# Linear attention into an MLP on one core: a rebuilt front, and every attention step placed by itself

## The chip, the cores and the metric

The kernel runs on one core of a Trainium2 chip. The metric is device time in microseconds, as the median of several runs. The profile shows one execution. Its engines are TensorE (PE for matmuls, PEld for loading weights), VectorE (DVE), ScalarE (ACT), GpSimd (POOL) and SyncE (SP), which here only issues transfers. Each engine takes its instructions in the order in which the program lists them.

## What is computed

There are two parts, and the second takes the output of the first.

```python
def phi(x):                                        # S1, S2: 8 x 32
    a = np.einsum('rd,bhsd->bhsr', S1, x)
    b = np.einsum('rd,bhsd->bhsr', S2, x)
    return np.einsum('bhsi,bhsj->bhsij', a, b).reshape(*x.shape[:-1], 64)
q_p, k_p = phi(q), phi(k)                          # q, k, v: 4 x 4 x 1088 x 32
kv = np.einsum('bhsf,bhsd->bhfd', k_p, v)
z = np.sum(k_p, axis=2)
x = (q_p @ kv) / (q_p @ z + 1e-06)                 # then 4352 tokens x 128
h = x @ w_in                                       # 128 x 2048
out = (h * sigmoid(beta * h)) @ w_out              # 2048 x 128
```

## The kernel before

Attention is done batch by batch. For each of the four batches the steps are these, with the lines of the kernel before:

- `load_k`, `load_q`, `load_v`: transfers from DRAM. `hold` (L115) first writes one column of the target on an engine, which makes the transfer wait for that place in the program. All but the first k and beta are issued on SP.
- `k_turn` (L287) and `q_turn` (L293): VectorE transposes blocks of 32x32, so that the head dimension lies along partitions.
- `project` (L314 on TensorE, L323 on VectorE): the product with S1 and S2, then a transpose back into a tile `ab`.
- `k_product` (L343): the 64 features of k, shared between VectorE and GpSimd.
- `v_copy` (L304): v with a column of ones, for kv and z at once.
- `kv` (L362), `kv_spread` (L372, L376), `weights` (L386, L394), `kv_repeat` (L403 on TensorE, L411 on ScalarE): the sums over all tokens, brought into the shapes that the later products need.
- `den_product`, `den_invert`, `weigh` (L418 on TensorE, L428 to L462 on VectorE): the denominators, and a tile `an` of q's first factor divided by them.
- `q_multiply` (L479) and `q_back` (L487), for three thirds (`ch` 0, 1, 2): the 64 features of q, then a transpose.
- `num_part` (L498), and the copies of its result into `x_all` (L556), two on VectorE and two on ScalarE.

The sequence is divided into 34 units of 32 tokens in each batch. The MLP (`moe`) takes ten chunks of 12, 11, 11, six times 16, and 6 units. A chunk runs as a series of waves: two matmuls with `winp` (L605) fill a pair of PSUM banks, ScalarE applies Silu to both (L612) into `gT`, and two waves later two matmuls with `woutp` (L581) add to the output (four and four for the last chunk). There are two pairs of banks, so wave n+2 needs the pair that ScalarE has read for wave n. There are 76 waves; here they are counted from 0. Chunks 0 to 2 (waves 0 to 23) belong to batch 0, and batch 1 must be ready for wave 24, batch 2 for wave 40, batch 3 for wave 56. `winp` is w_in times beta and `woutp` is w_out over beta; GpSimd makes them in steps of two blocks (L255, L264).

Batch 0 is written out ahead of the waves, with its own form of the first third: its numerator is formed undivided (`num_first`) and multiplied by the reciprocals later (`quotient`, L530, L539), so that wave 0 needs one third of the batch alone. Between the steps stand idle matmuls on a zero tile (`warm`, L210). The later batches' steps are attached to waves by number: `at_wave(n, f)` puts f behind wave n in the program. Most steps come in groups, for example

```python
at_wave(w0 + proj_k, *((a.v_copy,) if b > 1 else ()), a.k_project, a.k_product)
at_wave(w0 + wt, a.weights, a.kv_repeat)
at_wave(w0 + den, a.weigh)
at_wave(w0 + n0, lambda a=a: a.num_part(0, NCH, EV))
```

No scheduler moves anything: this order is what each engine runs.

Of the kernel before, what the change touches and what calls it, by code (L numbers as in the profile page):

```python
# [7 lines left out]
F32 = mybir.dt.float32  # L8
F16 = mybir.dt.float16
ALU = mybir.AluOpType  # L10
# [8 lines left out]
def kernel(  # L19
# [32 lines left out]
    assert U == 34  # L52
# [45 lines left out]
    s16 = const.tile([2 * R, D], F32, tag="s16")  # L98
# [8 lines left out]
    nc.scalar.dma_start(out=k_in[0], in_=k_rows[0])  # L107
    nc.sync.dma_start(out=s16[0:R, :], in_=S1)
    nc.sync.dma_start(out=s16[R : 2 * R, :], in_=S2)
    nc.scalar.dma_start(out=beta4[0:P:T, :], in_=moe_beta.rearrange("(i n) -> i n", n=512))  # L110
    nc.sync.dma_start(out=q_in[0], in_=q_rows[0])
# [5 lines left out]
    def load_w_in(eng):  # L117
        hold(eng, w_in_sb)
        nc.sync.dma_start(out=w_in_sb, in_=moe_w_in)
        nc.sync.dma_start(out=betat, in_=moe_beta.rearrange("(p j) -> p j", j=NJ))  # L120
# [5 lines left out]
    def load_k(b, eng):  # L126
        hold(eng, k_in[b])
        nc.sync.dma_start(out=k_in[b], in_=k_rows[b])
# [29 lines left out]
    for h in range(H):  # L158
        nc.gpsimd.memset(hmask[T * h : T * h + T, h % 2, :], 1.0)

    j8 = const.tile([2 * R, P // R, R], F32, tag="j8")
    nc.gpsimd.memset(j8, 1.0)
    nc.gpsimd.affine_select(
        out=j8, in_=j8, pattern=[[0, P // R], [-1, R]], base=-R, channel_multiplier=1,
        compare_op=ALU.is_equal, fill=0.0,
    )
# [6 lines left out]
    load_v_late(0, nc.gpsimd)  # L173
# [32 lines left out]
    idle_out = bank("acc")  # L206

    def warm(n):
        for _ in range(n):
            nc.tensor.matmul(out=idle_out, lhsT=idle[:, 0:P], rhs=idle, start=True, stop=True)  # L210
# [7 lines left out]
    def sketches():  # L218

        w = bank("att")  # L220
        for h in range(H):
            nc.tensor.matmul(
                out=w[T * h : T * h + T, 0 : 2 * R], lhsT=s16, rhs=idf[0 : 2 * R, 0 : 2 * R], start=True, stop=True
            )
        nc.vector.tensor_tensor(
            out=apx(wab, 0, [[2 * R, 2], [1, 2 * R]]),
            in0=apx(w, 0, [[0, 2], [1, 2 * R]]),
            in1=hmask,
            op=ALU.mult,
        )  # L230
        w = bank("att")
        nc.tensor.matmul(out=w[:, 0:D], lhsT=j8.rearrange("k x r -> k (x r)"), rhs=s16, start=True, stop=True)
        nc.scalar.copy(out=s2rep, in_=apx(w, 0, [[0, H], [1, D]]))
# [6 lines left out]
    def beta_rows():  # L240

        for i in range(2):
            w = pair()
            for k_ in range(2):
                p0 = T * (2 * i + k_)
                nc.tensor.matmul(
                    out=w[:, k_, :], lhsT=ones[p0 : p0 + 1, :], rhs=beta4[p0 : p0 + 1, :], start=True, stop=True
                )
            nc.scalar.copy(
                out=beta_bc[:, 1024 * i : 1024 * i + 1024].rearrange("q (k n) -> q k n", k=2), in_=w  # L250
            )

    def scale_w_in(j0, j1):
        for j in range(j0, j1, 2):
# [3 lines left out]
                in1=apx(beta_bc, j, [[1, 2], [NJ, P]]),  # L258
                op=ALU.mult,
            )  # L260

# [15 lines left out]
    class Attention:  # L277
# [5 lines left out]
        def k_turn(self, halves=(0, 1)):  # L283
            half = U // 2 + 1
            for i in halves:
                u0, u1 = ((0, half), (half, U))[i]
# [10 lines left out]
        def v_copy(self):  # L297
            if self.first:
                parts = ((nc.scalar.copy, 0, 2), (nc.scalar.copy, 2, H))
            else:  # L300
                parts = ((nc.gpsimd.tensor_copy, 0, H),)
            for f, h0, h1 in parts:
                for p1, c0, c1 in ((P, 0, NL), (T * (NS - 1), NL, C)):
                    f(  # L304
                        out=self.vc[0:p1, c0:c1, h0:h1, 0:D].rearrange("p c h d -> p h c d"),
                        in_=v_in[self.b][0:p1, h0:h1, c0:c1, :],
                    )
# [438 lines left out]
```

## Time and profile before

| What | Value |
|---|---|
| Median of 3 runs | 112.78 us (112.75 to 115.35) |
| Profiled execution: its own time | 112.65 us |
| its span (first to last instruction) | 110.8 us |
| TensorE matmul busy | 101.1 us, 91% |
| VectorE busy | 69.5 us, 63% |
| ScalarE busy | 75.7 us, 68% |
| GpSimd busy | 30.7 us, 28% |
| Mean granted clock of TensorE | 0.985 |

The time of the profiled execution is 1.85 us more than its span, which begins with the first instruction and ends with the last. TensorE's busy time is large in part because matmuls overlap and idle matmuls count as well. Stages are therefore read from tables by stretch and from the chain of work that ended last, which goes back from the last instruction, each time to what released it.

Some durations that are needed below, as means of one instruction: L612 at 1024 columns 1059 ns, 704 columns 756 ns, and in sequence about 0.1 us less each, since they overlap; L343 on GpSimd 1067 ns for 512 elements and 3061 ns for 768; L479 about 930 ns; L487 974 ns; L255 1070 ns; L264 622 ns; L293 1305 ns.

### The profile page before, as it was taken

What the parts mean: (1) busy time and instruction counts of PE and PEld (TensorE: products, weight loads), DVE (VectorE), ACT (ScalarE), POOL (GpSimd) and SP (SyncE); (2) the same over time, 40 slices, a digit from 0 to 9 for tenths busy, and PEclk for the clock granted to TensorE, in tenths of its full rate; (3) what the DMA queues carried; (4) which work ended last, traced back from release to release, by engine and by line L of the source; (5) the groups of instructions that cost most, each with busy time, mean ns of one, the idle gap of its engine ahead of it and who ended that gap; (6) DMA issues with size and microseconds to landing.
All of it is one profiled execution on the core that took longest, in us unless ns stands there. A gap on an engine that the chain in (4) does not pass through costs nothing.

```text
span 110.8 us, 3276 instructions
## 1 busy us (share of the span) xinstructions
PE 101.1 (91%) x1385; PEld 49.5 (45%) x1385; DVE 69.5 (63%) x137; ACT 75.7 (68%) x105; POOL 30.7 (28%) x54
## 2 busy tenths in 40 slices
PE   5999796987988999899999999999999999999950
PEld 2332763334456555444734443365444444444640
DVE  5269775899998799579769965933998220020110
ACT  1608411292753799479569976856999799999940
POOL 6503197899580003228000040920000000000000
PEclk9999999599999999999999999999999999999999
DMA  3899139997001342249401506060000056004153
GB/s 91 261 264 313 65 62 400 387 268 272 11 0 24 53 131 70 37 64 356 90 6 35 167 3 101 0 92 9 0 0 0 16 85 96 1 12 65 24 74 56
DMA packets 22119, 11.25 MB, mean 101 GB/s; under 512 B 18772, under 2 KB 20820, under 8 KB 21848
## 3 DMA queue, kind: packets, MB, share of 16 engines
q1 hardware_dynamic: 21536, 10.42, 37.3%
q10 hardware_dynamic: 568, 0.61, 1.8%
q8 instruction: 11, 0.18, 0.7%
q14 instruction: 4, 0.03, 0.1%
HBM read 8.80 MB, written 2.23 MB: 99 GB/s over the span
## 4 chain that ended last, share of the span: by engine, by line
PE 39%; DVE 28%; ACT 18%; DMA 5%; issue 2%; POOL 2%; SPq 1%; ACTq 0%; POOLq 0%; DVEq 0%
ACT gT L612 17%; PE wave L605 10%; PE acc L581 9%; DVE qpt L487 8%; DVE qp L479 6%; DMA v_in<-in_v_dram 5%; PE wave L498 4%; PE att L418 3%; PE att L314 2%; PE att L362 2%; PE att L403 2%; PE wave L362 2%; DVE kp L343 2%; DVE den L444 2%; PE att L498 1%
## 5 line engine op out<-in xcount | busy, mean ns | idle before, releaser
L612 ACT ACTIVATE gT<-wave 128x1024 f16<-128x1024 f32 (+2 forms) x76 | 65.1, 958 | 11.7 <-PE wave L605 11.6
L605 PE MATMUL wave<-x_all,winp 128*128 128x512 f16 (+3 forms) x160 | 42.5, 353 | 0.3 <-ACT gT L612 0.3
L581 PE MATMUL acc<-gT,woutp 128*128 128x512 f16 (+3 forms) x160 | 41.7, 347 | 0.2 <-ACT gT L612 0.2
L605 PEld LDWEIGHTS <-winp 128*128 128x128 f16 x160 | 14.2, 99 | 21.6 <-issue 13.0
L581 PEld LDWEIGHTS <-woutp 128*128 128x128 f16 x160 | 15.3, 97 | 14.4 <-issue 0.4
L586 DVE STREAM_TRANSPOSE osb<-acc 128x512 f32<-128x512 f32 (+3 forms) x10 | 6.2, 618 | 16.8 <-PE acc L581 16.8
L343 POOL TENSOR_TENSOR kp<-ab 128x768 f32<-128x768 f32 (+1 forms) x4 | 10.3, 2563 | 13.1 <-DVE ab L323 13.1
L487 DVE STREAM_TRANSPOSE qpt<-qp 128x768 f32<-128x768 f32 x12 | 11.7, 974 | 0.4
L304 POOL COPY vc<-v_in 128x896 f32<-128x896 f32 (+1 forms) x6 | 4.2, 740 | 22.3 <-DMA v_in<-in_v_dram 22.3
L210 PE MATMUL acc<-idle 128*128 128x512 f16 x23 | 8.3, 500 | 1.3 <-DVE idle L145 1.3
L498 PE MATMUL wave<-qpt,kvw 32*32 32x288 f32 (+2 forms) x192 | 6.9, 344 | 1.9 <-DVE qpt L487 1.9
L479 DVE TENSOR_TENSOR qp<-an,ab 128x768 f32<-128x768 f32 x9 | 8.4, 930 | 0.1
L255 POOL TENSOR_TENSOR winp<-w_in_sb,beta_bc 128x256 f16<-128x256 f32 x8 | 8.4, 1070 | 0.0
L323 DVE STREAM_TRANSPOSE ab<-att 128x288 f32<-128x288 f32 x16 | 6.6, 453 | 2.3 <-PE att L314 2.3
L343 DVE TENSOR_TENSOR kp<-ab 128x1536 f32<-128x1536 f32 (+2 forms) x5 | 7.3, 1481 | 0.2
L287 DVE STREAM_TRANSPOSE kT<-k_in 128x576 f32<-128x576 f32 (+1 forms) x8 | 5.5, 717 | 1.9 <-DMA k_in<-in_k_dram 1.8
L411 ACT COPY kvw<-att 128x128 f32<-128x128 f32 x8 | 2.1, 267 | 6.3 <-PE att L403 5.9
L556 ACT CAST x_all<-att 128x288 f16<-128x288 f32 (+1 forms) x8 | 2.6, 382 | 5.4 <-PE att L498 5.4
L556 DVE CAST x_all<-wave 128x288 f16<-128x288 f32 (+1 forms) x8 | 3.1, 428 | 4.6 <-PE att L498 4.6
L498 PE MATMUL att<-qpt,kvw 32*32 32x288 f32 (+1 forms) x128 | 6.0, 392 | 0.0
L498 PEld LDWEIGHTS wave<-qpt,kvw 32*32 32x32 f32 x192 | 3.8, 103 | 4.6 <-ACT gT L612 3.3
L293 DVE STREAM_TRANSPOSE qT<-q_in 128x1088 f32<-128x1088 f32 x4 | 5.2, 1305 | 0.1
(85 smaller groups left out, 76.1 us busy)
## 6 DMA issues: line engine op xcount, KB each, us to landing
q_in<-in_q_dram SPq DMA_DIRECT2D x4, 544.0 KB, 6.6
v_in<-in_v_dram SPq DMA_DIRECT2D x12, 144.0 KB, 5.7
k_in<-in_k_dram SPq DMA_DIRECT2D x3, 544.0 KB, 4.1
w_in_sb<-in_moe_w_in_dram SPq DMA_DIRECT2D x1, 1024.0 KB
w_out_sb<-in_moe_w_out_dram SPq DMA_DIRECT2D x1, 1024.0 KB, 4.8
out_dram<-osb SPq DMA_DIRECT2D x16, 64.0 KB, 2.0
k_in<-in_k_dram ACTq DMA_DIRECT2D x1, 544.0 KB, 3.6
v_in<-in_v_dram SPq DMA_DIRECT2D x4, 112.0 KB, 4.3
```

Of the source, the lines that this page charges most:

```text
L210: nc.tensor.matmul(out=idle_out, lhsT=idle[:, 0:P], rhs=idle, start=True, stop=True)
L255: nc.gpsimd.tensor_tensor(out=winp[:, j : j + 2, :], in0=apx(w_in_sb, j, [[1, 2], [NJ, P]]), in1=apx(beta_bc, j, [[1, 2], [NJ, P]]), op=AL ...
L323: nc.vector.transpose(out=apx(ab, T * p, [[2 * T, C], [1, T]]), in_=banks[p][:, 0 : C * T])
L343: eng.tensor_tensor(out=apx(self.kp, c0 * H * F, [[F, n], [R, R], [1, R]]), in0=apx(t, c0 * H * 2 * R, [[2 * R, n], [1, R], [0, R]]), in1= ...
L479: nc.vector.tensor_tensor(out=apx(self.qp, 0, [[F, n], [R, R], [1, R]]), in0=a, in1=apx(self.ab, c0 * H * 2 * R + R, [[2 * R, n], [0, R], ...
L487: nc.vector.transpose(out=apx(self.qpt, ch * CW * T, [[T, CW], [C * T, 2 * H], [1, T]]), in_=self.qp.rearrange("p n f -> p (n f)"),)
L498: nc.tensor.matmul(out=dst[T * h : T * h + T, 0:n], lhsT=self.kvw[T * s : T * s + T, h % 2, fb, h // 2, :], rhs=self.qpt[T * s : T * s + T ...
L556: copies[e](out=x[:, :, s * CT : (s + 1) * CT], in_=src.rearrange("p (c n) -> p c n", n=CT))
L581: nc.tensor.matmul(out=acc[:, :n], lhsT=woutp[:, j, :], rhs=gT[:, j, :n], start=(j == 0), stop=(j == NJ - 1))
L586: nc.vector.transpose(out=osb[:, :un, :].rearrange("p u m -> p (u m)"), in_=acc[:, :n])
L605: nc.tensor.matmul(out=wave[:, jj // (nj // 2), jj % (nj // 2) * n : (jj % (nj // 2) + 1) * n], lhsT=winp[:, j0 + jj, :], rhs=x, start=Tru ...
L612: nc.scalar.activation(out=gT[:, j0 : j0 + nj, :n].rearrange("p (i k) n -> p i k n", i=2), in_=wave[:, :, : nj // 2 * n].rearrange("p i (k ...
```

## The change

The front:

- S1 and S2 are brought in by two transfers that repeat the 8 rows over all 128 partitions. A transpose on VectorE and a product with the mask then give `wab`. The matmuls that did this (L222, L232) and the tile `j8` are gone.
- The first k is loaded in halves on SP, followed by q and v on the same queue; v no longer waits for a mark on GpSimd. ScalarE's queue issues S and beta. The first half of batch 1's k is also loaded early, ahead of w_in; the other half later.
- Idle matmuls have 320 columns in place of 512, and their numbers change. The 192 columns left free in that PSUM bank take the rows of batch 0's second denominator.
- `project` runs in two parts for batch 0's k. `k_product` is called for each engine by itself; batch 0's q transpose stands between the two VectorE parts.
- Batch 0's v is copied on ScalarE (units 0 to 3) and GpSimd (4 to 8), all heads at once.
- The copies of beta are laid out so that GpSimd reads them contiguously; ScalarE reads PSUM with a stride for that.
- `q_back(0)` is done before `kv_spread`. `kv_repeat` is split around the new `den_rows`, which is the matmul part of `den_product`. `num_first` and `quotient` go by pairs of banks. Half of batch 1's k transpose stands in the front.
- Eight of the sixteen `woutp` blocks are made on ScalarE, two each after waves 1 to 4.

The later steps: a table `plan` gives every step of every batch a place of its own, and a step with value p stands behind wave floor(p), in the order of the values. `num_part` is divided into the matmuls and `evacuate`. Batch 1's second `q_multiply` runs on GpSimd. Batch 0's last copies go three to ScalarE and one to VectorE (`AVAA`).

```diff
+    UH = U // 2 + 1
+    nc.sync.dma_start(out=k_in[0][:, 0 : UH * D], in_=k_rows[0][:, 0 : UH * D])
+    for i, s_ in enumerate((S1, S2)):
+        nc.scalar.dma_start(
+            out=s12[:, i, :], in_=bass.AP(tensor=s_.tensor, offset=s_.offset, ap=[[0, P // R], [D, R], [1, D]])
+        )
+    nc.sync.dma_start(out=k_in[0][:, UH * D : U * D], in_=k_rows[0][:, UH * D : U * D])
+    nc.sync.dma_start(out=q_in[0], in_=q_rows[0])
     nc.scalar.dma_start(out=beta4[0:P:T, :], in_=moe_beta.rearrange("(i n) -> i n", n=512))
-    nc.sync.dma_start(out=q_in[0], in_=q_rows[0])
+    load_v(0)
...
+    NI = 512 - 2 * CT
     def warm(n):
         for _ in range(n):
-            nc.tensor.matmul(out=idle_out, lhsT=idle[:, 0:P], rhs=idle, start=True, stop=True)
+            nc.tensor.matmul(
+                out=idle_out[:, 0:NI], lhsT=idle[:, 0:P], rhs=idle[:, 0:NI], start=True, stop=True
+            )
...
+        st = const.tile([P, 2, T], F32, tag="st")
+        nc.vector.transpose(out=st.rearrange("p i r -> p (i r)"), in_=s12.rearrange("p i d -> p (i d)"))
...
+        nc.scalar.copy(
+            out=apx(beta_bc, i * half, [[P, NJ], [1, half]]),
+            in_=apx(beta_ps[i], 0, [[1, NJ], [NJ, half]]),
+        )
...
+    def scale_w_out_act(j):
+        nc.scalar.activation(out=woutp[:, j, :], in_=w_out_sb[:, j, :], func=ACTF.Copy, scale=rbetat[:, j : j + 1])
...
-    warm(9)
+    warm(15)
     a0.k_turn((0,))
     sketches()
-    warm(2)
+    a0.k_project((0, 1))
+    load_k(1, nc.vector, 0, UH)
+    load_w_in()
+    warm(1)
     a0.k_turn((1,))
-    load_w_in(nc.vector)
-    a0.k_project()
+    a0.k_project((2, 3))
+    beta_rows(0)
+    beta_rows(1)
+    beta_copy(0)
+    warm(7)
+    a0.k_product(nc.vector, 0, 4)
+    hold(nc.vector, w_outf)
+    hold(nc.gpsimd, w_outf)
     a0.q_turn()
-    beta_rows()
-    warm(5)
-    a0.v_copy()
-    a0.k_product()
+    a0.k_product(nc.gpsimd, 7, C)
+    a0.k_product(nc.vector, 4, 7)
+    a0.v_copy(nc.scalar.copy, ((0, 4),))
+    a0.v_copy(nc.gpsimd.tensor_copy, ((4, 7), (7, 9)))
+    beta_copy(1)
     a0.q_project()
-    warm(3)
+    warm(4)
     a0.kv((0, 1))
     a0.q_multiply(0)
-    hold(nc.vector, w_outf)
-    hold(nc.gpsimd, w_outf)
+    load_w_out(nc.vector)
+    a0.q_back(0)
     scale_w_in(0, 10)
+    warm(2)
+    load_k(1, nc.vector, UH, U)
     a0.kv_spread()
-    load_w_out(nc.vector)
-    warm(2)
+    load_q(1, nc.vector)
     a0.weights()
-    a0.kv_repeat()
...
+    a0.kv_repeat((0,))
+    a0.den_rows(0, 1)
+    a0.kv_repeat((1,))
+    at[1].k_turn((0,))
     a0.den_product(0, 1)
     a0.den_invert(0, 1, rz[:, :, 0:H])
     a0.spread_rden()
+    nc.vector.reciprocal(out=rbetat, in_=betat)
+    a0.num_first()
+    warm(3)
+    a0.quotient()
     load_v_late(1, nc.vector)
-    a0.num_first()
-    a0.quotient()
+    a0.den_rows(1, NCH, idle_out[:, NI:512])
+    warm(3)
     a0.den_product(1, NCH)
     a0.weigh(1)
-    warm(2)
     for j in range(10, NJ, 2):
         scale_w_out(j - 10, j - 8)
         scale_w_in(j, j + 2)
-    scale_w_out(NJ - 10, NJ)
-    at[1].v_copy()
...
+    slots = [(1.5 + (j - NJ // 2) // 2, -1, lambda j=j: scale_w_out_act(j)) for j in range(NJ // 2, NJ)]
+    plan = [
+        {"mul1": 0.1, "back1": 0.45, "mul2": 0.15, "back2": 0.5, "num": 4.05, "ev": 4.1},
+        {"turn_k": 0.6, "proj_k": 5.1, "vcopy": 0.1, "kp_pool": 7.5, "turn_q": 1.6, "kp": 5.75, "proj_q": 7.3, "kv0": 9.1, "kv1": 9.5, "spread": 9.6, "weights": 9.65, "repeat": 10.5, "den": 10.15, "inv": 10.2, "mul0": 13.45, "back0": 16.1, "mul1": 17.2, "back1": 19.8, "mul2": 17.55, "back2": 19.85, "num": 22.9, "ev": 22.95},
+        {"load_k": 1, "load_q": 1.05, "load_v": 13.3, "turn_k": 8.1, "turn_q": 10.55, "vcopy": 23.4, "proj_k": 20.95, "kp_pool": 24.4, "kp": 21.7, "proj_q": 23.6, "kv0": 25.05, "kv1": 25.25, "spread": 25.6, "weights": 26.05, "repeat": 31.1, "den": 28.9, "inv": 29.4, "mul0": 29.85, "back0": 32.3, "mul1": 30.5, "back1": 32.35, "mul2": 32.95, "back2": 35.7, "num": 38.5, "ev": 38.85},
+        {"load_k": 16, "load_q": 21.1, "load_v": 32.2, "turn_k": 26.6, "turn_q": 24.85, "vcopy": 39.6, "proj_k": 33.75, "kp_pool": 36.6, "kp": 39, "proj_q": 39, "kv0": 41.25, "kv1": 41.9, "spread": 41.95, "weights": 43.3, "repeat": 45.5, "den": 44.05, "inv": 46.65, "mul0": 46.7, "back0": 48.75, "mul1": 47.75, "back1": 50.8, "mul2": 49.8, "back2": 51, "num": 54, "ev": 54.95},
+    ]
...
+            "ev": lambda a=a, b=b: a.evacuate("VVAA" if b else "AVAA"),
...
+            do[f"mul{ch}"] = lambda a=a, ch=ch, e=nc.gpsimd if b == 1 and ch == 1 else None: a.q_multiply(ch, e)
...
     n = 0
     for u0, un in chunks:
         for _ in moe(u0, un):
-            for f in slots.get(n, ()):
-                f()
             n += 1
+            while slots and slots[0][0] < n:
+                slots.pop(0)[2]()
     flush(0)
```

In the kernel before, the places of the later batches in the same counting were: batch 1: k turn 2, proj_k 5, proj_q 7, kv and weights with repeat 9, denominators 10, q's products 14, numerator 22. Batch 2: proj_k 23, proj_q 25, kv 27, weights with repeat 28, denominators 29, q's products 32, numerator 38. Batch 3: proj_k 39, proj_q 41, kv 43, weights with repeat and denominators 44, q's products 46 and 48, numerator 54.

## The prediction

> **What bounds the kernel now.** I read the slices of the span first, to see where the clock or the transfers are unusual; then the chain that ended last, for who sets the time; then tables of busy time by stretch, for what each stage could still give.
>
> ```profile
> PEclk9999999599999999999999999999999999999999
> DMA  3899139997001342249401506060000056004153
> ...
> 10.76 1.25 ACT vc L304 x3
> 12.01 0.04 issue
> 12.05 2.17 PE wave L362 x68
> ...
> 18.52 0.37 DVE x_all L539
> 18.89 0.04 issue
> 18.93 0.83 PE att L418 x8
> 19.78 0.41 DVE acc L428
> ...
> 24.61 0.99 DVE qpt L487
> 25.60 0.14 issue
> 25.73 0.35 PE wave L498 x2
> ```
>
> In the chain (start, length, what) the reader sees a front of 25.7 us that is one string of small steps: v lands at 10.7, ScalarE copies it, TensorE forms kv until 14.2, the first third of x_all is ready at 19.14, VectorE then needs four denominator steps, two products and two transposes (L479, L487) before the second numerator can start. Wave 0 of the MLP starts at 20.5, but that doesn't set the end: after five waves TensorE waits for VectorE.
>
> ```profile
> 15.64:19.05 3.41, 2.27 (x86) 1.50 (x88) 2.44 (x9) 0.89 (x4) 2.94 (x3) 1.00 0.95 333
> 19.05:22.46 3.41, 3.15 (x15) 1.03 (x13) 2.63 (x9) 1.08 (x2) 2.77 (x4) 0.50 1.02 377
> 27.00:45.00 18.00, 16.95 (x271) 9.45 (x276) 16.66 (x28) 13.41 (x22) 6.30 (x6) 1.00 0.20 48
> 48.00:65.20 17.20, 17.09 (x241) 8.02 (x234) 14.88 (x25) 14.12 (x17) 4.27 (x3) 1.00 0.42 115
> 68.40:85.80 17.40, 17.40 (x254) 8.18 (x255) 12.98 (x21) 14.03 (x18) 3.09 (x1) 1.00 0.13 20
> ```
>
> Columns: stretch, length, then busy time of PE, PEld, DVE, ACT, POOL, then granted clock, DMA share, GB/s. For 3.4 us TensorE has half its clock, after a stretch in which it was busy 2.27 of 3.41. The three long rows are the stages of batches 1, 2 and 3. In the first VectorE is at 16.66 of 18.0 and TensorE still has holes; in the other two TensorE is full. Behind 87.9 ScalarE alone is the limit (21 activations back to back, 18.65 us), and the change leaves those 21 waves as they are: the last numerator stands behind wave 54 in both kernels. So only what comes before 85.8 counts.
>
> **The change part by part.** All sums are against the profiled execution: 112.65, of which 110.8 is span and 1.85 lies around it; that is 0.13 under the median of 112.78.
>
> *k chain.* S no longer goes through TensorE (8 and 2 instructions, and VectorE's 0.40 wait); a transpose of 128x64 (about 0.2, by the 128x96 row at 0.28) and the product (0.19) replace them. The first half of k should land near 3.3 instead of 4.47 (half of the 2.3 us that the whole took after its first bytes). Turn 0.78, transpose, product: wab at 4.5. The 15 idle matmuls at half clock (320 columns, 0.27 each by 0.447 for 512) hold TensorE until 5.3, so project starts there instead of 6.31, and its two transposes end at 7.25 instead of 8.13: -0.9. VectorE now does the first k product (1.18) before the q transpose (1.30), so that q's landing at 8.2 is hidden, then the second (0.95): done 10.7 instead of 11.5.
>
> *v.* It is issued at about 2 to 4 us instead of 3.30 to 5.20 (its third and fourth piece wait on SP for S and the first half of k, which land near 3.3: the transfers share eight completion semaphores). Does it land earlier? The DMA share was 0.82 from 3.5 to 5.5 and 1.03 from 5.5 to 8.2, so little of the line is free: bounds are 10.72 (no gain) and 9.2 (all of the 1.5 us). I take 10.4, nearer the first. The copy is 512 elements on ScalarE (0.63, by 0.57 for 448) beside 384 and 256 on GpSimd (0.5 and 0.40), instead of 1.44 in sequence. kv can start at 11.05, where q's projection and four idle matmuls end as well, and lasts 2.25: end 13.3 instead of 14.23, **-0.9** (-0.3 to -1.0).
>
> On this the Trainium skill speaks against the change: "DMA: Bandwidth & Descriptors", section "Issuing engines are not separate DMA queues", says that transfers of all queues share the same 16 engines and that another issuer saves issue time alone. By it the landing stays at 10.7 and the total is 0.3 higher.
>
> *kv to x_all.* q_back(0) (0.92) now ends at 13.4, before kv_spread, and leaves the string; but the first half of batch 1's k turn (0.78) stands before the denominator's transpose. It fills the wait for den_rows almost wholly (+0.2). Numerator, three idle matmuls (0.4) and quotient follow: 4.8 us as before: 4.9. x_all at 18.1, **-1.05**. SP's queue gains one issue of 0.35 (k in halves); w_out is issued at 12.5 instead of 14.79, behind w_in. w_in moves behind 295 KB of k: lands near 14.2 instead of 12.95. GpSimd needs five scalings from there (1.07 each before; with beta now contiguous between 0.62, the woutp row, and 1.07) and ends at 17.3 to 19.6, while waves ask for them from 18.5 at 0.74 apart: hidden, with about 2 us to spare. The strided PSUM read of the beta copy has no row: between 1.0 and 2.0; ScalarE has both free.
>
> *x_all to the second numerator.* The 0.64 wait of L428 for L418 goes: den_rows is placed before and, with idle matmuls, at full clock (192 columns took 0.81 at half). The rest is the same string, 1.95 + 3.85: numerator at 23.95 instead of 25.73, **-1.8**. Eight woutp scalings move to ScalarE, about 0.27 each, in waves 1 to 4, where ScalarE waits for the numerator. The copies AVAA put three on ScalarE (0.95 instead of 0.54) and give back 0.3: proj_k at 26.15 instead of 27.69, **-1.5**.
>
> *Batch 1.* proj_k, transposes to 27.6, GpSimd's k product 3.06 to 30.7, kv to 31.75 (33.82). VectorE: k turn of batch 2 and osb to 32.1, zi to wc 32.9, then a hole until wave 10 and den_rows (33.9), five steps to 36.4, q turn 1.30 (it lay in a wait before; now it is in the string), then mul0, back0, osb, mul2, back1, back2: 5.3. GpSimd's mul1 (between 1.6, by 1.07 for 512, and 3.06) is ready at 39.5 and takes 0.92 off VectorE. Numerator at 43.1 instead of 44.94: **-1.85**. But VectorE then holds proj_k's transposes (0.85) and kp (1.76) of batch 2 ahead of its two copies of x_all, which wait to 46.45. TensorE reaches wave 24 at 46.5 instead of 47.98: **-1.5**.
>
> *Batches 2 and 3.* TensorE is full there. A step placed alone costs 0.11: the wave behind an attention step takes 0.54 in the chain, others 0.43. Batch 2's stage changes proj_q for batch 3's proj_k and has one step more (+0.11); the 0.15 wait for back2 at 65.1 goes. Batch 3's loses proj_k (0.65 + 0.11) and has two steps more (+0.22): -0.54. Moved pieces bring nothing else, since each goes from one full stage to another.
>
> Sum: -1.5 + 0.11 - 0.15 - 0.54 = -2.08. 112.65 - 2.08 = **110.6**. About 2% (2.26 us) is what a measurement of this kernel can tell from no change, so the forecast lies at that edge.
>
> **Rivals.**
> *A, the middle closes up.* If GpSimd's products take 1.6 instead of 3.06 and VectorE is never late, batch 1's stage is TensorE's own work: 15.3 us of matmuls and seven switches from 26.15, the numerator at 42.2, copies in time. 0.9 + 0.4 more: 109.3. For it: GpSimd's 512 elements took 1.07 in the front. Against: its three later products all took over 3 us, with VectorE busy.
> *B, ScalarE and TensorE set batch 1.* Thirteen waves at ScalarE's 0.665, with 2.2 us of steps and their switches between, put the numerator at 44.1, not 43.1: 111.6. For it: the steps are alone, so nothing overlaps them.
> *C, slower: the clock.* TensorE idles from 8.4 to 9.75 in the new front (waiting for the q transpose) and a little before kv. If a 3.4 us window there holds no more than the 2.27 busy us that preceded half clock (2.60 from 8.81 to 12.22 did not), kv, weights, repeats and den_rows run at half speed: 2.25 + 0.4 = 2.7 late, 113.3. Against: the idle matmuls, and VectorE may start earlier.
>
> The Trainium skill ("TensorE: Matmul & The Clock Gate", section "What's actually happening") has the clock halve after an idle window of 3.4 us. The row differs: 2.27 busy us were not enough. By the rule C can't happen; by the row it can, and I go by the row.
>
> That the change doesn't do what it says I exclude for the order: the new program has each step where the diff says. For the clock I don't.
>
> **How the numbers follow.** Forecast 0.45 (109.8 to 111.4, a little over half of it under 110.5), A 0.27, B 0.16, C 0.12. Faster by over 2%: 0.24 + 0.26 = 0.50. Slower by over 2% (115.0): 0.04, from C with a second lost window. Within: 0.46. The range 109.0 to 112.9 leaves out the far part of A (0.09) and of C (0.08).
>
> **What would show it.** L361 ends near 13.3 after v's landing at 10.4; the first x_all near 18.1; L436 right behind its transpose, with no wait for L417; the second numerator at 24; no half clock from 19 to 22; the numerators of the three later batches at 43, 64 and 83.7; ScalarE's tail still 18.65. I am wrong if the first of these is not earlier, if POOL's winp holds the waves, or if VectorE's kp of batch 2 delays wave 24 by more than 0.4.

## The result, and the profile after

The change made the kernel slower: 122.27 us as the median of five runs (122.05 to 123.84), against 112.78 before. The ratio is 1.0875, with an interval of 1.0783 to 1.0967. Some executions of one kernel take over 1.5% longer than its fastest; the ratios here leave these out, while medians and ranges are over all. The forecast was 110.6, and 122.27 lies far outside its range. The profiled execution took 122.27 with a span of 120.5.

Starts of the numerators in the two profiles, from TensorE's timeline, say where the time went:

| Numerator | before | after | difference |
|---|---|---|---|
| batch 0, second and third part | 25.73 | 35.45 | +9.72 |
| batch 1 | 44.94 | 56.46 | +11.52 |
| batch 2 | 65.25 | 75.99 | +10.74 |
| batch 3 | 85.72 | 95.36 | +9.64 |

The front lost 9.7 us. Batch 1 lost another 1.8, and batches 2 and 3 gave back 0.8 and 1.1. ScalarE's tail is 18.65 us in both. So nearly everything was lost before 35 us. The chain of work that ended last, of the changed kernel (start, length, what):

```profile
0.81 2.97 DMA s<-in_S_dram
3.79 4.12 DMA v_in<-in_v_dram
7.92 0.04 issue
7.96 0.26 DVE st L221
...
8.55 1.18 PE att L315 x8
...
13.25 1.98 PE acc L208 x7
15.23 1.28 PE att L315 x16
16.51 0.84 DVE ab L326 x2
17.37 3.67 DVE qp L481
...
24.17 1.82 PE wave L501 x58
...
28.81 0.93 PE acc L208 x3
29.76 0.41 DVE acc L431
...
35.31 0.14 issue
35.45 0.35 PE wave L501 x2
```

In place of "v lands, copies, kv" the front begins with S. VectorE's transpose of S (L221) waits until 7.96. The chain names v's transfer for the wait up to then, but S shares a completion semaphore with a piece of v. ScalarE, which reads S at L228, waits for it just as long (first line, from the timeline), and the view of the tile of S tells when it landed:

```profile
7.88 0.30 ACT L228 COPY s2rep<-s 128x128 f32<-128x128 f32 x1 [2.46 <-DMA s<-in_S_dram]
...
L111 ACTq DMA_DIRECT2D s<-in_S_dram x2: 616/635/654, 0.8 to 1.5; - x2
...
DMA to landing us min/median/max: 3.0/4.7/6.4
```

The two issues on ScalarE's queue start at 0.8 and 1.5, and the slower of them lands 6.4 us after its issue, at 7.9. I had taken S to be there by about 4.

The second thing to see in the chain is 3.67 us for the first q product (L481), which took 0.96 in before. The third is the clock. From the slices of the span:

```profile
PEclk9999999855999999999999999999999999999997
DMA  3778400691606304088503026304100502303234
```

There are two slices at half clock (24 to 30 us), and the first change to full clock that the trace records comes only at 16.65, where before had it at 5.40. The row shows nothing of the time ahead of the first record, but durations do. The 16 matmuls of q's projection, in the timelines of TensorE, first of the changed kernel, then of before:

```profile
15.16 1.21 PE L315 MATMUL att<-qT,wab 64*32 64x288 f32 x16
```

```profile
9.68 0.72 PE L314 MATMUL att<-qT,wab 64*32 64x288 f32 x16 [0.21 <-DVE qT L293]
```

The reason is in the table by stretch (stretch, length, busy time of PE, PEld, DVE, ACT, POOL, clock, DMA share, GB/s): TensorE has nothing to do from 5.44 to 8.55, as it waits for `wab`. The last three rows answer those of the three later batches.

```profile
3.00:6.41 3.41, 2.44 (x10) 1.06 (x7) 0.78 (x1) 2.19 (x4) 0.76 (x5) 1.00 0.78 271
6.41:9.83 3.41, 1.27 (x9) 0.31 (x9) 1.07 (x4) 0.30 (x1) 0.00 (x0) 1.00 0.67 155
```

```profile
39.00:56.50 17.50, 15.18 (x258) 8.42 (x258) 15.41 (x28) 11.46 (x19) 4.30 (x4) 1.00 0.42 109
59.00:76.00 17.00, 17.00 (x252) 7.69 (x242) 13.23 (x24) 14.33 (x18) 2.23 (x3) 1.00 0.29 62
79.00:95.40 16.40, 16.40 (x233) 7.55 (x228) 11.37 (x19) 14.02 (x18) 0.00 (x0) 1.00 0.17 26
```

In batches 2 and 3 TensorE is full, as in before, and from numerator to numerator they are shorter. In batch 1 TensorE has 2.3 us of holes.

### The profile page after: what moved, and what is told of

The parts are those of the page before. It is cut to its first block, busy times and chain, and to the rows that moved or that the text cites. A ratio compares the mean times of both kernels' runs of the same rounds, so it can differ in the third digit from the quotient of the medians.

```text
span 120.5 us, 3284 instructions
## 1 busy us (share of the span) xinstructions
PE 105.0 (87%) x1387; PEld 51.3 (43%) x1387; DVE 71.4 (59%) x136; ACT 77.2 (64%) x111; POOL 25.6 (21%) x50
## 4 chain that ended last, share of the span: by engine, by line
PE 58%; ACT 16%; DVE 15%; DMA 6%; issue 1%; DVEq 0%
PE wave L612 17%; ACT gT L619 15%; PE acc L588 15%; PE att L315 6%; PE wave L501 5%; DVE qp L481 5%; PE acc L208 3%; DMA v_in<-in_v_dram 3%; DMA s<-in_S_dram 2%; PE att L403 2%; DVE kp L342 2%; DVE qpt L489 2%; PE att L361 2%; DVE ab L326 2%; PE wave L242 2%; PE att L417 2%
## 5 line engine op out<-in xcount | busy, mean ns | idle before, releaser
L342 POOL TENSOR_TENSOR kp<-ab 128x768 f32<-128x768 f32 (+1 forms) x4 | 7.1, 1776 | 20.6 <-DVE ab L326 19.8
L489 DVE STREAM_TRANSPOSE qpt<-qp 128x768 f32<-128x768 f32 x12 | 11.2, 956 | 0.1
L208 PE MATMUL acc<-idle 128*128 128x320 f16 x35 | 9.9, 446 | 1.3 <-DVE idle L150 1.3
L501 PE MATMUL wave<-qpt,kvw 32*32 32x288 f32 (+2 forms) x192 | 7.8, 381 | 1.4 <-DVE qpt L489 1.4
L342 DVE TENSOR_TENSOR kp<-ab 128x1536 f32<-128x1536 f32 (+2 forms) x5 | 8.4, 1678 | 0.6 <-DVE ab L326 0.5
L481 DVE TENSOR_TENSOR qp<-an,ab 128x768 f32<-128x768 f32 x8 | 7.6, 976 | 0.1
L208 PEld LDWEIGHTS <-idle 128*128 128x128 f16 x35 | 4.1, 133 | 8.0 <-issue 4.2
L315 PE MATMUL att<-kT,wab 64*32 64x288 f32 x64 | 4.6, 482 | 3.1 <-DVE k_in L121 3.1
L303 POOL COPY vc<-v_in 96x256 f32<-96x256 f32 (+2 forms) x8 | 5.5, 719 | 6.2 <-DMA v_in<-in_v_dram 6.2
L256 POOL TENSOR_TENSOR winp<-w_in_sb,beta_bc 128x256 f16<-128x256 f32 x8 | 6.6, 841 | 0.0
```

What stands on the lines that cost most here:

```text
L208: nc.tensor.matmul(out=idle_out[:, 0:NI], lhsT=idle[:, 0:P], rhs=idle[:, 0:NI], start=True, stop=True)
L256: nc.gpsimd.tensor_tensor(out=winp[:, j : j + 2, :], in0=apx(w_in_sb, j, [[1, 2], [NJ, P]]), in1=apx(beta_bc, j * P, [[P, 2], [1, P]]), op ...
L315: nc.tensor.matmul(out=banks[p][T * s : T * s + T, 0 : C * T], lhsT=wab[64 * p : 64 * p + 64, :], rhs=apx(src[64 * p : 64 * p + 64], s * s ...
L342: eng.tensor_tensor(out=apx(self.kp, c0 * H * F, [[F, n], [R, R], [1, R]]), in0=apx(t, c0 * H * 2 * R, [[2 * R, n], [1, R], [0, R]]), in1= ...
L481: (eng or nc.vector).tensor_tensor(out=apx(qp, 0, [[F, n], [R, R], [1, R]]), in0=a, in1=apx(self.ab, c0 * H * 2 * R + R, [[2 * R, n], [0, ...
L489: nc.vector.transpose(out=apx(self.qpt, ch * CW * T, [[T, CW], [C * T, 2 * H], [1, T]]), in_=self.qp[ch].rearrange("p n f -> p (n f)"),)
```

## The experiments

The theory: S lands late because its 256 rows of 128 bytes share the DMA engines with rows of 1 to 4 KB. That lateness moves the q product behind the start of GpSimd's scalings of `winp`, and the two exclude each other. The rivals are the clock, the layout of beta, and a new front that is slow by itself.

Where no ratio is given, the runs were too few or too scattered for one.

| Kernel | median (range), us | ratio to before [interval] |
|---|---|---|
| changed | 122.27 (122.05 to 123.84) | 1.0875 [1.0783, 1.0967] |
| S first | 117.43 (116.20 to 122.19) | 1.0417 [1.0315, 1.0518] |
| holds behind the product | 117.82 (116.91 to 121.14) | 1.0483 [1.0410, 1.0556] |
| S first, holds behind | 114.42 (112.18 to 119.53) | 1.0009 [0.9954, 1.0064] |
| beta as before | 124.19 (123.01 to 124.88) | 1.1044 [1.0957, 1.1130] |
| 32 idle matmuls | 122.78 (122.60 to 123.21) | 1.0958 [1.0915, 1.1001] |
| 32 idle matmuls, holds behind | 116.25 (115.11 to 120.54) | 1.0318 [1.0213, 1.0422] |
| S as before | 114.95 (111.33 to 117.91) | none |
| S as before, holds behind | 113.72 (112.59 to 116.17) | 1.0071 [1.0006, 1.0137] |
| new front, old places | 117.77 (114.47 to 121.34) | 1.0260 [1.0100, 1.0420] |
| old front, new places | 111.72 (110.59 to 112.88) | 0.9907 [0.9857, 0.9957] |
| q transpose first | 113.32 (112.87 to 115.19) | 1.0027 [0.9961, 1.0094] |
| 20 idle matmuls in the gap | 119.31 (114.90 to 121.65) | none |
| q first, 13 idle matmuls | 113.87 (111.90 to 118.09) | none |
| old front, new places, v and denominators | 111.04 (109.39 to 114.86) | 0.9739 [0.9628, 0.9850] |
| old front, new places, v | 111.93 (109.84 to 114.38) | none |

### S first

```diff
-    nc.sync.dma_start(out=k_in[0][:, 0 : UH * D], in_=k_rows[0][:, 0 : UH * D])
     for i, s_ in enumerate((S1, S2)):
-        nc.scalar.dma_start(
+        nc.sync.dma_start(
...
+    nc.sync.dma_start(out=k_in[0][:, 0 : UH * D], in_=k_rows[0][:, 0 : UH * D])
```

> S1 and S2 are issued on SP ahead of the first k, the same 128-byte rows; nothing else changes. Theory late S: in the changed kernel the transpose of S waits until 7.96, k's projection starts at 8.55 instead of 6.31, and the half clock and the 3.67 us product follow from that. Then S lands near 3, projection starts near 5.5, batch 0's first q product comes near 12, ahead of GpSimd's scalings of w_in, and takes about 0.95; x_all near 18.5; total 111 to 113. Rival, the product is slow by itself (GpSimd's contiguous scalings): the product stays near 3.7 and only the earlier start is won: 117 to 118. Rival, the clock of TensorE doesn't come up in the new front whatever S does: project stays at 1.2 us for 8 matmuls, total 118 to 119.

It came to 117.43, half of the loss gone. In the view of the tile of S:

```profile
DMA to landing us min/median/max: 2.3/2.3/2.4
```

The same rows, issued before the large transfers instead of beside them, land 2.3 us after issue instead of up to 6.4. So it isn't the transfer as such that is slow, but its place; queue and order changed together here, and which of them counts isn't shown. The rows count too: in the run with S as before and the holds behind (below), two loads of 8 rows on ScalarE's queue, beside the same large ones, are in use by TensorE at 4.86. The early place has a price all the same: each of the two issues held SP for 0.7 us, and the first half of k landed at 5.48 instead of 3.61.

### The holds behind the product

```diff
     a0.k_product(nc.vector, 0, 4)
-    hold(nc.vector, w_outf)
-    hold(nc.gpsimd, w_outf)
     a0.q_turn()
...
     a0.q_multiply(0)
+    hold(nc.vector, w_outf)
+    hold(nc.gpsimd, w_outf)
     load_w_out(nc.vector)
```

> The two marks on w_out stand behind the first q product again, as in the kernel before, so that GpSimd's scalings of w_in wait for that product. Theory exclusion: L481 takes 0.95 instead of 3.67; TensorE's idle time before L385 shrinks by 2.7 and its second half clock (23.5 to 30.3) goes or gets shorter; total 117 to 119.5. Rival, the product is slow for another reason (ScalarE's beta copy, transfers): L481 stays over 3 us and the total at 122.

117.82, within what was expected. `hold` on `w_out` writes a column first on VectorE, then on GpSimd, and GpSimd's waits for VectorE's. Behind the q product, it keeps GpSimd's five scalings behind the product too. The changed kernel moved the two holds ahead of the q transpose, and so dropped an order that nothing else enforced. From the timelines of VectorE and GpSimd (start, length, engine, line), the changed kernel first, then this run:

```profile
16.17 4.06 POOL L256 TENSOR_TENSOR winp<-w_in_sb,beta_bc 128x256 f16<-128x256 f32 x5
...
17.37 3.67 DVE L481 TENSOR_TENSOR qp<-ab 128x768 f32<-128x768 f32 x1
```

```profile
16.64 0.96 DVE L481 TENSOR_TENSOR qp<-ab 128x768 f32<-128x768 f32 x1
...
17.68 0.10 POOL L121 MEMSET w_out_sb<- 128x1 f32 x1 [2.55 <-DVE w_out_sb L121]
17.77 4.09 POOL L256 TENSOR_TENSOR winp<-w_in_sb,beta_bc 128x256 f16<-128x256 f32 x5
```

In the changed kernel the product begins inside the scalings and ends at 21.04, 0.81 us after the last of them (20.23). It waits until all five are done, then runs at about its usual speed. The Trainium skill ("SBUF — State Buffer", section "Who interferes with whom") states this: a VectorE instruction with two SBUF inputs contends with a GpSimd instruction that reads SBUF, the pair of ports goes to whichever starts first for its whole instruction, and "Issue order, not op shape, decides who blocks." The rows agree, with 3.67 against 0.96. They add that back-to-back GpSimd instructions can keep the product out for their whole length. They need not: in the profile with S first the product came in after the one scaling that was running, and ended 0.81 after that one (15.96), and the second scaling took 1.57 instead of 0.84. What decides between the two was not tried. From the timeline of that run:

```profile
15.12 4.81 POOL L256 TENSOR_TENSOR winp<-w_in_sb,beta_bc 128x256 f16<-128x256 f32 x5 [0.71 <-DMA w_in_sb<-in_moe_w_in_dram]
15.58 1.20 DVE L481 TENSOR_TENSOR qp<-ab 128x768 f32<-128x768 f32 x1
```

Before's later products (L479 at 21.76, 0.96 us) ran beside scalings unhindered; their first input lies in PSUM.

### Both

> S issued first on SP, by the same repeated rows, and the guard. S first alone gave 117.4, 4.7 over before, with S landed at 3.9 but the first half of k at 5.48 instead of 3.61. Theory (in those runs the q product met the scalings as well, which the guard takes away): 114 to 115.5. Rival (the two issues of 0.7 on SP put k, q and v 1.5 to 1.9 later, and that is passed on whole, the product being a minor part): 116.3 to 117.5.

The median lies in the theory's range, the four of its ten runs that the ratio rests on below it (112.18 to 113.41); the ratio, 1.0009, says that in these the whole loss is gone. Alone, the holds bring the ratio down by 0.039 and S first by 0.046; the sum would leave 1.0025. So the loss divides into some 5 us for S and 4.4 us for the missing order, and the two add up. By this sum the product still waited for the scalings in the runs of S first alone; that is argued, and not shown: in its one profile, of the run of 122.19, the product lost only 0.24.

### Beta as before

```diff
-            out=apx(beta_bc, i * half, [[P, NJ], [1, half]]),
-            in_=apx(beta_ps[i], 0, [[1, NJ], [NJ, half]]),
+            out=beta_bc[:, 1024 * i : 1024 * i + 1024].rearrange("q (k n) -> q k n", k=2), in_=beta_ps[i]
...
-                in1=apx(beta_bc, j * P, [[P, 2], [1, P]]),
+                in1=apx(beta_bc, j, [[1, 2], [NJ, P]]),
```

> Beta's copies and the scalings of w_in have their old layout (strided read on GpSimd, 1.07 us each instead of 0.84). Theory exclusion: a VectorE product with two SBUF inputs waits until GpSimd's row of scalings that read SBUF is over, whatever their layout; five of them now end later, so L481 grows to about 4.8 and the total goes to 123 to 124. Rival, contiguous reads of beta are what shuts VectorE out: L481 returns to 0.96 and the total goes to 117 to 119.

124.19: the strided read makes a scaling 1.07 us instead of 0.84, and the product is held longer by it:

```profile
16.94 5.17 POOL L254 TENSOR_TENSOR winp<-w_in_sb,beta_bc 128x256 f16<-128x256 f32 x5
...
18.14 4.78 DVE L479 TENSOR_TENSOR qp<-ab 128x768 f32<-128x768 f32 x1
```

Scalings end at 22.11, the product at 22.92: again 0.81 later. The new layout is no cause; the ratios (1.1044 here, 1.0875 with it) speak for a gain, though their intervals overlap a little.

### Idle matmuls, alone and with the holds

```diff
-    warm(15)
+    warm(32)
     a0.k_turn((0,))
```

> 32 idle matmuls instead of 15 ahead of k's projection, to keep TensorE busy while S is awaited. Theory clock: the half clock from 5.4 to 16.65 comes from TensorE's idle 3.1 us there; with it gone k's projection takes 0.45 and 0.45 instead of 1.18 and 1.19, beta's rows 1.14 instead of 2.09, and q's projection starts near 13 instead of 15.2: total 116 to 120, the lower if the first q product then comes ahead of the scalings of w_in. Rival, the clock is a side effect and VectorE's waits set the front: less than 1 us, 121.3 to 122.5.

122.78, no gain. The clock was full from 5.86 to 22.92 and the k projection took 0.69 a half instead of 1.18. But the product, now started at 16.28, took 4.55 and ended at 20.83, at the same place as before the edit: the scalings had swallowed it all. With the holds back the clock had a price of its own:

> The changed kernel with 32 idle matmuls in place of 15 and with the guard (the two holds on w_out behind the first q product); S still by the repeated rows. The 32 alone gave nothing, while the q product took 4.55 among the scalings. Theory (the clock is worth something once the product no longer meets the scalings): k's project at 8.6 to 9.5 and 0.7 a half, q's projection 0.85, the product 0.96, first x_all at 22.5 to 23.3, time 115.5 to 117.0, against 117.8 for the guard alone. Rival (the string goes through S's landing and VectorE, the clock doesn't matter): 117.3 to 118.5.

1.0318, against 1.0483 with the holds alone: about 1.9 us, though the two intervals overlap a little. So the clock was probably a cause too, hidden behind a larger one.

### S as before, without and with the holds

```diff
-    for i, s_ in enumerate((S1, S2)):
-        nc.scalar.dma_start(
-            out=s12[:, i, :], in_=bass.AP(tensor=s_.tensor, offset=s_.offset, ap=[[0, P // R], [D, R], [1, D]])
-        )
+    nc.scalar.dma_start(out=s16[0:R, :], in_=S1)
+    nc.scalar.dma_start(out=s16[R : 2 * R, :], in_=S2)
```

with the matmuls of before in `sketches`.

> The changed kernel with S brought in as before: two loads of 8 rows and the matmuls that spread them, nothing else changed. Theory (the broadcast rows of S are late, and all that follows in the front comes from it): S lands near 2.5, k's project starts near 5.5 instead of 8.55, the first q product runs near 13 and takes about 0.95 because it comes ahead of GpSimd's five scalings (w_in lands behind 14), the first x_all is at 18 to 19.5, and the time is 110.5 to 113.5, the front's 9.7 us gone. Rival (the new front is slow by itself, in its transfers or its order): S is early, but x_all stays at 22 or later and the time at 116 or more. Rival (exclusion without the late S): the product meets the scalings all the same and takes over 3 us; 113.5 to 116.

> As the run with S of before, and the two holds on w_out stand behind the first q product again, so that GpSimd's scalings of winp come after it. Theory: the product takes 0.96 whatever w_in's landing is; the time is the same as without the holds within 0.7 if the product was ahead of the scalings there, and up to 3 us less if it met them: 110.5 to 113. Rival (scalings that start later make the waves wait for winp): 0.5 to 2 us more than without the holds.

The first gave four runs, 111.33, 113.14, 116.76 and 117.91, too scattered for a ratio. In its profile the product stood at 13.30 with 0.96 us and the scalings at 14.00: with S early the order that the holds enforced comes out by itself, by 0.7 us. With the holds, 1.0071. So the rest of the new front brings no gain, where the forecast had 1.5 us; against the new places on the old front (0.9907, below) it costs some 1.8 us. The timeline of TensorE with the holds shows why:

```profile
5.50 0.98 PE L324 MATMUL att<-kT,wab 64*32 64x288 f32 x8
6.41 0.31 PE L212 MATMUL acc<-idle 128*128 128x320 f16 x1
6.65 0.69 PE L324 MATMUL att<-kT,wab 64*32 64x288 f32 x8
...
10.89 1.10 PE L324 MATMUL att<-qT,wab 64*32 64x288 f32 x16 [1.42 <-DVE qT L305]
11.93 1.25 PE L212 MATMUL acc<-idle 128*128 128x320 f16 x4
13.11 2.91 PE L370 MATMUL wave<-vc,kp 128*64 128x33 f32 x72
```

The project began at 5.50, 0.8 us earlier than in before, but in two parts it took 1.84, where the 16 matmuls in one took 0.89. VectorE's first k product then began at 8.30, and before had its q transpose at 8.22. With the product ahead of it the q transpose stood at 9.44. TensorE idled 1.42 for it, and in the table by stretch that is followed by half clock into kv:

```profile
7.68:11.09 3.41, 1.99 (x23) 0.82 (x23) 3.38 (x5) 1.01 (x1) 2.10 (x1) 1.00 1.06 263
11.09:14.50 3.41, 3.41 (x46) 1.83 (x32) 2.69 (x7) 1.53 (x2) 1.09 (x4) 0.50 0.49 191
```

That is rival C of the prediction, in its place and by its row, once S is early: 1.99 busy us of 3.41, and half clock after it.

### One half of the change at a time

Old front, new places: loads, S, beta, idle matmuls and order up to the waves from before, the rest from after. New front, old places: the kernel of the last run, with the later steps grouped as before.

> Before's front (loads, S, beta, idle matmuls, order) with the single places of the later steps, the three copies on ScalarE and the second q product of batch 1 on GpSimd. Theory (the plan is neutral: 1.85 lost in batch 1 to VectorE's product of k waiting for GpSimd's, 1.9 gained in batches 2 and 3): 112 to 113.2. Rival (the plan loses 2 or more by itself, since its batch 1 only came out well because all was late): 114.5 or more. Rival (the plan gains what I forecast for the later batches, 0.6, and batch 1's loss came from the half clock and the late front): 110.3 to 111.8.

> The changed front with S and the holds as before, and the later steps in the groups of before (copies and products on the engines of before). Theory (the rest of the new front is worth what I forecast for v, kv and the denominators, about 1 to 1.8, and the groups pass it on): 110.8 to 112. Rival (the front's gain is lost again before the second numerator, as batch 1 is set by VectorE): 112.2 to 113. Rival (the new front without the broadcast is still slower than before's): over 113.

The places alone are a small gain, 0.9907 and 111.72, in the range of the last rival. But that rival laid batch 1's loss to the late front, and batch 1 still loses here. The numerators of that run start at 25.16, 45.28, 64.82 and 84.19: batch 1 took 20.1 us from numerator to numerator (19.2 in before), batches 2 and 3 took 19.5 and 19.4 (20.3 and 20.5). The new front without the new places is the slower half (114.47 to 121.34), as the second rival had it. Its profile, of the run of 121.34, has half clock from 11.39 to 28.46.

### The q transpose first, and the gap filled

```diff
-    a0.k_product(nc.vector, 0, 4)
     a0.q_turn()
+    a0.k_product(nc.vector, 0, 4)
```

> The run with S and the guard as before (113.72, 0.8 over before), with batch 0's q transpose ahead of VectorE's first product of k, as before has it; nothing else. In that run the q transpose started at 9.44 (8.22 in before) because the 1.22 us product came first, TensorE idled 1.42 for it, kv started at 13.11 and half clock lay on 11.09 to 14.50. Theory (this order is what is left of the loss): the q transpose starts at 8.3 to 8.8 (q lands 8.5 to 8.7), q's projection at 9.8 to 10.2, kv at 12 to 12.3, behind v's landing of 11.0 to 11.4, kv ends near 14.4, x_all at 18.6 to 19.2, and the time is 111.3 to 112.6. Rival (v's later landing and the copies set kv, not q): kv starts at 12.8 or later, 113 to 114. Rival (the clock alone): the order is as expected, but half clock falls into kv again, over 113.

> The run with S and the guard as before, with 20 idle matmuls instead of 7 ahead of q's projection, so that TensorE doesn't idle while it waits for the q transpose; the order is unchanged. Theory of the clock: no half clock from 11 to 14.5; q's projection 0.72 instead of 1.10, the four idle matmuls 0.65 instead of 1.18, kv 2.2 instead of 2.84, together 1.5 earlier at kv's end where the clock was halved: 112 to 113, and less spread between runs than 112.6 to 116.2. Rival (the order, not the clock): under 0.4 us gained, 113.3 or more.

> Both edits: the q transpose ahead of VectorE's first product of k, and 13 idle matmuls in place of 7 ahead of q's projection. If order and clock are separate causes: 0.3 to 1 us under the run with the order alone, 111 to 112.3, and no half clock before 17. If they are one cause (the gap that the order makes is what halves the clock): the same as the order alone within 0.3.

The order first, on S as before with the holds: 1.0027, and 1.0071 without the edit; the intervals overlap. The profile moved as expected, except for the transfers: the q transpose waited for q until 8.98, and v was copied at 11.74. So kv ran from 12.42 to 14.71, later than in before. The new order of loads doesn't bring v earlier.

With twenty idle matmuls in the gap the times went up, 114.9 to 121.65. The chain of its profile, in which the clock was at half until 16.57:

```profile
11.28 5.43 PE acc L212 x20
16.71 0.78 PE att L324 x16
17.50 0.84 DVE ab L335 x2
18.36 0.96 DVE qp L490
```

At half clock the twenty take 5.43 us, and q's projection, whose transpose was done at 12.66, waits behind them for 4 us. A fixed number of idle matmuls is right for one clock only. Both edits together gave 111.9 to 118.09, and no ratio: whether order and clock are one cause stays open.

### The best of both

The old front with the new places, v copied on ScalarE and GpSimd at once, and `den_rows` ahead, into the idle bank. The idle matmuls have 320 columns for that, and more of them stand in most places (15 instead of 9 at the start):

```diff
-    for h0, h1 in ((0, 2), (2, H)):
-        for p1, c0, c1 in ((P, 0, NL), (T * (NS - 1), NL, C)):
-            nc.scalar.copy(
-                out=a0.vc[0:p1, c0:c1, h0:h1, 0:D].rearrange("p c h d -> p h c d"),
-                in_=v_in[0][0:p1, h0:h1, c0:c1, :],
-            )
+    a0.v_copy(nc.scalar.copy, ((0, 4),))
+    a0.v_copy(nc.gpsimd.tensor_copy, ((4, 7), (7, 9)))
...
-    a0.den_rows(1, NCH)
+    a0.den_rows(1, NCH, idle_out[:, NI:512])
+    warm(3)
```

> The front of before in its order, with the single places of the later steps (that alone gave 0.9907), and two pieces of the new front put into it: batch 0's v copied on ScalarE and GpSimd at the same time, and the matmuls of the second denominator ahead of the wait, on 192 columns of the idle bank, with idle matmuls of 320 columns. Theory: kv starts at 10.9 to 11.5 with v's landing at 10.2 to 10.7 and ends 0.5 earlier than with the plan alone; the wait of VectorE for the denominator's matmuls (0.65) goes; both pass to the second numerator: 110.0 to 111.0. Rival (batch 1 is set by VectorE and GpSimd, not by the front): the same as the plan alone within 0.3.

The four runs were 109.39, 110.43, 111.66 and 114.86, and the ratio rests on the first two: 0.9739, with an interval of 0.9628 to 0.9850, faster than both kernels. A gain of 2% is likely and not certain. With v alone:

> Before's front with the single places of the later steps, and batch 0's v copied on ScalarE and GpSimd at the same time; the denominators as before. The plan alone gave 0.9907, with the two pieces (v and the early denominator matmuls) 0.974. If v is worth about half of the difference: 0.980 to 0.985, kv ends 0.5 earlier than with the plan alone (13.67 there). If all of it came from the denominators: 0.988 to 0.993. If all came from v: 0.972 to 0.978.

It gave 109.84 to 114.38 and no ratio, so how much each piece is worth stays open. In its profile v was worth what was expected (kv ended at 13.19, against 13.67 with the places alone), and the second numerator started at 24.19, 1.0 earlier. Not all of that is v's: the run with the places alone had half clock from 17.55 to 20.97, and this one none there. Batch 1's numerator then started only 0.45 earlier, and batch 2's 0.7 later. From the timelines of VectorE and GpSimd, with the places alone first, then with v:

```profile
43.94 1.28 POOL L299 COPY vc<-v_in 128x896 f32<-128x896 f32 x2 [4.38 <-ACT gT L615]
...
45.31 1.76 DVE L338 TENSOR_TENSOR kp<-ab 128x1536 f32<-128x1536 f32 x1
...
45.42 3.01 POOL L338 TENSOR_TENSOR kp<-ab 128x768 f32<-128x768 f32 x1 [0.20 <-DVE q_in L117]
```

```profile
43.90 1.29 POOL L299 COPY vc<-v_in 128x896 f32<-128x896 f32 x2 [4.78 <-ACT gT L615]
...
44.86 3.41 DVE L338 TENSOR_TENSOR kp<-ab 128x1536 f32<-128x1536 f32 x1
...
45.15 1.50 POOL L338 TENSOR_TENSOR kp<-ab 128x768 f32<-128x768 f32 x1
```

VectorE came 0.45 us earlier, found GpSimd still at its copy of v, and was shut out by that and by the product behind it: 3.41 us instead of 1.76. Here an earlier VectorE is a later one.

## Why the prediction was wrong, point by point

- **"The k chain", -0.9: the step that failed.** "wab at 4.5" rested on S being there, and S had been given no price as a transfer. It was 256 rows of 128 bytes beside large rows, landed at 7.9, and cost some 5 us with what hung on it (S first). Even with S early the term was nil: in two parts the projection took 1.84 instead of 0.89, and VectorE was ready at 8.30 instead of 8.22.
- **"Hidden, with about 2 us to spare", the second failed step.** I asked whether the scalings would be late for the waves. I didn't ask who shares something with them: the q product had been kept ahead of them by the holds, which the diff shows as moved and which I priced at nothing. With S late the product came at 17.37 into scalings from 16.17: 3.67 instead of 0.96, and 4.4 us of the time by the runs. The 0.92 to 0.96 that I carried over for the products came from rows where the partner wasn't reading at the same time, or where one input lay in PSUM.
- **v at 10.4:** v landed at 10.85, and in the six runs with the new loads and S as before its first copy began at 10.40 to 12.22; with the old loads it began at 10.04 to 10.76. No gain, or a loss; the bound with no gain was the right one.
- **"kv can start at 11.05":** in the run with S and the holds as before it started at 13.11, from the q transpose, the clock and four idle matmuls. With the q transpose first it was 12.42.
- **The second denominator's wait (0.64):** it didn't go, it changed its object. `den_rows` now writes into the bank of the idle matmuls, and VectorE's L431 starts at 29.76, right after the three idle matmuls that follow (28.81, 0.93 us), not after L417. (The string behind it was also summed 0.15 short: from 19.78 to 25.73 before takes 5.95, not 1.95 + 3.85.)
- **Batch 1:** from numerator to numerator I had 19.15 us; it was 21.0 in the changed kernel, 20.1 with the old front. GpSimd's k product started at 39.32, 0.38 ahead of VectorE's, which took 2.74 instead of 1.76. In before VectorE was 0.11 ahead, and paid nothing. With the old front it was 0.11 ahead again (28.92), and with the new one in two runs (S as before and S first, each with the holds); there batch 1 took 20.1, 19.7 and 19.9. So some 1 us of the 1.8 goes with that order, and the 0.5 to 0.9 that are left against before stay open. The lines of the changed kernel, then of before:

```profile
39.32 1.51 POOL L342 TENSOR_TENSOR kp<-ab 128x768 f32<-128x768 f32 x1 [5.07 <-DVE ab L326]
...
39.70 2.74 DVE L342 TENSOR_TENSOR kp<-ab 128x1536 f32<-128x1536 f32 x1 [0.53 <-DVE ab L326]
```

```profile
29.61 1.76 DVE L343 TENSOR_TENSOR kp<-ab 128x1536 f32<-128x1536 f32 x1
29.72 3.02 POOL L343 TENSOR_TENSOR kp<-ab 128x768 f32<-128x768 f32 x1 [1.11 <-DVE ab L323]
```

- That also settles rival A's term: GpSimd's 3 us are 1.5 of work and 1.5 of waiting (`mul1` on GpSimd, with no product of VectorE's ahead of it, took 1.51 at 49.23), so "between 1.6 and 3.06" was one size with and without VectorE ahead.
- **VectorE's kp of batch 2 ahead of the x_all copies (+0.35):** it stood ahead, but cost only 0.1; it was over as the numerator ended (58.06), and VectorE's copies start at 58.16.
- **Batches 2 and 3:** right in sign, too small. I had -0.04 and -0.54; between numerators they gained 0.8 and 1.1. The places alone are the part of the change that works; which of them brings this wasn't tried.
- **Rival C** was the right mechanism, with two mistakes. Its gap in the changed kernel was 3.1 us of waiting for `wab`, ahead of the one that I named, and I gave it no more than 2.7 us. The gap that I did name halved the clock in the run with S early. The Trainium skill ("TensorE: Matmul & The Clock Gate", "What's actually happening") asks for an idle window; here half clock followed 1.99 busy us of 3.41, and the measurement decides.

## What to carry to other kernels

Give every new transfer a landing time, by its row count and by what is issued beside it, before anything is built on it: the same 16 KB landed 2.3 or 6.4 us after issue, by its place. When a hold or a wait is moved, list what it kept apart, not only what it loaded; a VectorE product with two SBUF inputs beside a row of GpSimd instructions is such a pair, and the one that starts second, by 0.11 us in one case here, waits for the other, at worst for the whole row. Where two losses lie on one string, undoing one can show nothing (32 idle matmuls: no gain) and be worth something once the other is gone (about 1.9 us), so undo them in pairs.

## What the runs showed that I had not expected

- A VectorE product waited for a whole row of five back-to-back GpSimd instructions, and ended 0.81 us after the last of them, in the changed kernel, with beta as before and with 32 idle matmuls alike (4.06, 5.17 and 4.07 us of scalings). With S first it came in after one. Between GpSimd's two copies of v a VectorE product came in as well: with the holds behind the product, the second product of k, from 13.83, took 1.04, and the second copy 1.13, where the same copy took 0.40 in the changed kernel.
- Issues that repeat 8 rows over 128 partitions held their queue for 0.62 to 0.79 us each. Loads of 8 rows took 0.37 and 0.29 on SP in before; on ScalarE's queue, with S as before, the first took 0.62 as well, and the second 0.30.
- All stretches between two changes of the clock in the traces are whole multiples of 3.41 us. The first full clock is recorded at 3.9 to 6.8 us in eleven of the seventeen profiles and at 14.0 to 17.1 in the other six. In windows of 3.41 us that end at a change or a whole number of windows ahead of it, it came after 2.65 busy us (old front, new places) and 2.84 (holds behind the product), and not after 2.44 (changed kernel). In the run with 20 idle matmuls TensorE was busy without a gap from 1.26 on, and the full clock came at 16.57 all the same; part of that time went to matmuls of 16 rows. In the best of both two such windows, busy throughout (3.88 to 10.71), brought no full clock either; it came at 14.12. What counts as busy for the clock was not tried.
